# Spreading the loads of x by a plan, and mixing two batches side by side in the first stretch of a fused FFT-mixing and feed-forward kernel

## The chip, the cores and the metric

The kernel runs on one core of one Trainium2 chip. Times are device microseconds (us) of one execution. PE is TensorE (matmul), DVE is VectorE, ACT is ScalarE, POOL is GpSimd, and SP is SyncE, which here only issues DMAs. PE writes its results to buffers in a memory called PSUM; an eviction is the copy out of such a buffer by ACT or DVE. The granted clock is the share of PE's full clock in the trace's clock record; half clock means 0.5.

## The reference, cut to what matters

```python
# x (8, 3008, 256); filt_r, filt_i (1505, 256); w_in (256, 2048); w_out (2048, 256); beta (2048,)
X = np.fft.rfft(x, axis=1)                        # along the 3008 positions
y = np.fft.irfft(X * (filt_r + 1j * filt_i), n=3008, axis=1)
h = y.reshape(24064, 256) @ w_in
g = h * (1 / (1 + np.exp(-beta * h)))             # Swish with a beta per feature
out = g @ w_out                                   # (24064, 256) f32
```

## The kernel before: the parts that the change and the argument touch

The feed-forward part is a loop of 47 blocks of 512 tokens times 16 slices of the hidden width: 752 steps. The mixing (the FFT filter, done as matmuls with tables) of batch b+1 is woven into the steps of the "stretch" in which batch b goes through the feed-forward. Stretch 0 is the first 80 steps. A plan says which step runs which piece.

```python
for s in range(len(steps) + LAG):                 # LAG = 2
    ... two matmuls hps <- y, win_sb (512 columns each); ACT: gT = Silu(hps)
    if s in plan:
        for go in plan[s]: go()                   # pieces of the mixing
    ... four matmuls acc <- gT, wout_sb of step s - LAG; after the last slice DVE copies acc, SP writes out
```

A batch's mixing has four parts, and between them the data goes out to DRAM and comes back in another order:

```python
def s1(b, i, on_act):          # 16 pieces: x times table t1, evicted, written to DRAM scratch d1
    ...
    evac(s["a1"][:, jj : jj + 2, :], ps[:KP], on_act)      # on ACT or on DVE
    if jj + 2 == JG:
        nc.sync.dma_start(s["d1r"][:, g * JG : (g + 1) * JG, :], s["a1"][:])
        if g == J // JG - 1 and b + 1 < B:
            xs[b + 1] = load_x(b + 1)             # 8 DMAs, issued by POOL: the next batch's x
def a2_read(b): ...            # d1 read back as a2, 4 DMAs of 384 KB
def s23(b, i): ...             # 14 pieces, 12 with a product with a2; 4 DVE multiplies; POOL adds p_t + q_t -> v_t;
                               # two pieces later the matmul with v_t, evicted by ACT to z, written to d2
def zz_read(b): ...            # d2 read back as zz, 4 DMAs of 384 KB
def last(b, g, i, on_act): ... # batches 0 and 1: zz times table t4 -> y (s4 and y_read for later batches)
```

The plan of stretch 0 (batch 1 is mixed, batch 2 is begun) and of the later ones:

```python
if w_ == 0:
    place(w_, 0.00, 0.125, u1(b, True), per=2)
    ...
    place(w_, 0.175, 0.175, [lambda b=b: a2_read(b)], per=9)
    place(w_, 0.275, 0.76, u23(b), True)          # True: keep off the borders of blocks
    ...
        place(w_, 0.77, 0.88, u1(b + 1, True), per=2)
    place(w_, 0.80, 0.80, [lambda b=b: zz_read(b)], per=9)
    spread(first_step[1] - 8, first_step[1] - 2, last_units(1, 0))
        at(first_step[1] - 3, lambda b=b: a2_read(b + 1))
else:
    place(w_, 0.03, 0.48, u23(b), True)
    place(w_, 0.525, 0.525, [lambda b=b: zz_read(b)], per=9)
        place(w_, 0.49, 0.63, u1(b + 1))
        ...
```

So x of the next batch is loaded as soon as the last mixing piece `s1` of this batch has been planned. That is just when `d1` is being written and read back, or `d2` is.

## Time and profile before

| | before |
|---|---|
| median of 4 runs | 823.24 us (820.24 to 823.55) |
| span of the profiled execution | 821.0 us |
| PE busy | 782.2 us (95%) |
| one feed-forward step, from the timeline | 0.87 us, times 752 = about 654 us |
| share of PE in the chain that ended last | 80% |

In these traces PE works in order, so a matmul that waits holds up all that follow: four `acc` matmuls stand behind the waiting one at 67.48 us in the timeline below. With PE this busy and its work unchanged, time can only be won where PE stands still or runs at half clock. Idle time of another engine matters only where PE waits for that engine.

The page's 40 slices (each about 20.5 us), kernel before. A digit is the busy share in tenths; PEclk is the granted clock in tenths, and DMA the mean busy share of the 16 DMA engines.

```profile
## 2 busy tenths in 40 slices
PE   7898897999899999999999999999999999999997
...
PEclk9999999999999999999999999999999999999999
DMA  9955239224971349722695128942287033450101
```

The DMA row has a peak in each stretch of about five slices. Between the peaks it falls to 1 to 3.

Who PE waited for, from 39.5 to 800 us, kernel before. Columns: the waiting instruction's tile and line, what released it, total us, times, longest us.

```profile
engine line waited for: us in total, times, longest us
PE ps_2998 L608 <- DMA zz<-d_1773: 3.8, 1, 3.8
PE ps_1159 L551 <- DMA a_1040<-d_805: 2.8, 1, 2.8
PE ps_2098 L551 <- DMA a_2020<-d_1772: 2.4, 1, 2.4
PE ps_1387 L583 <- POOL v_t L573: 2.0, 1, 2.0
PE ps_5539 L608 <- DMA zz<-d_4070: 1.7, 1, 1.7
PE ps_2005 L479 <- DMA zz<-d_806: 1.4, 1, 1.4
```

The three longest waits are for tiles that come back from DRAM: `zz` (line 608) and `a2` (line 551; the profile calls its tiles a_...). The fourth is for POOL's add of `v_t`.

The timeline of PE around the wait at 67.5 us, kernel before. Columns: start, duration (us), engine, line, operation; idle before it and what ended it stand in brackets.

```profile
64.36 0.33 PE L479 MATMUL ps_1153<-t_82,zz 96*128 96x94 bf16 x4
67.48 0.39 PE L551 MATMUL ps_1159<-a_1040,tx 128*128 128x256 bf16 x2 [2.79 <-DMA a_1040<-d_805]
67.71 0.84 PE L782 MATMUL acc<-wout_sb,gT 128*128 128x256 bf16 x4
68.34 1.06 PE L754 MATMUL hps<-y,win_sb 128*128 128x512 bf16 x2
```

After 2.79 us of standing, four `acc` matmuls take 0.84 us and then two `hps` ones 1.06 us. Elsewhere these groups take 0.60 and 0.59. The clock record of the trace says 0.5 for 3.41 us from 67.94 on, and again from 143.03 and from 211.30, at the waits that end at 142.6 and 211.5.

Why the tile is late is in the list of DMA issues, 36 to 72 us, kernel before. Columns: what, queue, count, size of one, us from issue to landing.

```profile
xg<-in_x_dram POOLq DMA_DIRECT2D x4, 320.0 KB, 7.8
...
a_1040<-d_805 SPq DMA_DIRECT2D x1, 384.0 KB, 10.1
```

A read-back of 384 KB takes over 10 us while POOL's load of x runs beside it. The Trainium skill, "DMA: Bandwidth & Descriptors", section "Issuing engines are not separate DMA queues", says that DMAs issued by different engines run on the same 16 DMA engines and interleave. This trace agrees: the two come from different queues (SP and POOL), and the same read for batch 2 takes 3.15 us for its first tile, issued at 139.4, after the last part of x for batch 3 has landed (136.3).

### The profile page before, as it was taken

The page shows a single profiled execution, that of the slowest core. Times are in us where ns is not written, and L with a number is a line of the kernel's source. Part 1 is how long each engine was busy: PE and PEld are TensorE (multiplying, and loading weights), DVE is VectorE, ACT ScalarE, POOL GpSimd, SP SyncE. Part 2 cuts the span into 40 slices and gives each one's busy share as a digit, 9 for nine tenths or more (in the row PEclk, how much of TensorE's full clock was granted, in tenths as well). Part 3 has the DMA queues.
Part 4 walks back from the last instruction along what each step waited for, and adds up shares of the span by engine and source line. Part 5 has one row for each costly group of instructions (what it writes and reads, how often), then busy time and mean ns, then how long its engine had stood idle before and what let it go on. Part 6 is the DMA issues. An engine that isn't in the chain of part 4 may idle for free.

```text
span 821.0 us, 14878 instructions
## 1 busy us (share of the span) xinstructions
PE 782.2 (95%) x5718; PEld 544.9 (66%) x5806; DVE 461.5 (56%) x702; ACT 600.0 (73%) x915; POOL 169.4 (21%) x195
## 2 busy tenths in 40 slices
PE   7898897999899999999999999999999999999997
PEld 4765665766467666777567766676666766666664
DVE  7845962796527966188553877458772792510101
ACT  6786786787477875778667886678767788677775
POOL 8471321232002320034100332013200231000000
PEclk9999999999999999999999999999999999999999
DMA  9955239224971349722695128942287033450101
GB/s 195 232 151 139 64 97 269 81 84 85 271 202 34 102 86 286 183 72 65 148 304 129 46 65 207 279 95 65 74 250 201 26 105 101 130 127 26 52 26 52
DMA packets 125224, 106.94 MB, mean 130 GB/s; under 512 B 41297, under 2 KB 111202, under 8 KB 125154
## 3 DMA queue, kind: packets, MB, share of 16 engines
q1 hardware_dynamic: 120066, 91.05, 37.9%
q0 software_dynamic: 5088, 14.95, 10.2%
q8 instruction: 45, 0.74, 0.4%
q14 instruction: 25, 0.20, 0.1%
HBM read 54.01 MB, written 56.10 MB: 134 GB/s over the span
## 4 chain that ended last, share of the span: by engine, by line
PE 80%; DMA 7%; DVE 6%; issue 2%; POOL 2%; ACT 2%; SPq 0%; DVEq 0%; POOLq 0%; ACTq 0%
PE acc L782 37%; PE hps L754 33%; DVE p_t L564 2%; DVE ost L794 1%; DMA d_1772<-a_1894 1%; DMA a_1040<-d_805 1%; POOL v_t L573 1%; DMA d_5338<-a_5341 1%; DVE q_t L572 1%; DMA d_4069<-a_4072 1%; DMA d_6604<-a_6607 1%; DMA zz<-d_1773 1%; DVE q_t L570 0%; PE psz L399 0%; DMA d_805<-a_942 0%
## 5 line engine op out<-in xcount | busy, mean ns | idle before, releaser
L763 ACT ACTIVATE gT<-hps,beta_sb 128x512 bf16<-128x512 f32 x752 | 516.7, 687 | 198.5 <-PE hps L754 176.1
L782 PE MATMUL acc<-wout_sb,gT 128*128 128x256 bf16 x3008 | 455.1, 273 | 3.2
L754 PE MATMUL hps<-y,win_sb 128*128 128x512 bf16 (+7 forms) x1641 | 431.5, 352 | 0.3 <-DVE y L98 0.2
L782 PEld LDWEIGHTS <-gT 128*128 128x128 bf16 x3008 | 291.8, 98 | 153.9 <-issue 2.8
L573 POOL TENSOR_TENSOR v_t<-p_t,q_t 128x512 bf16<-128x512 f32 x84 | 106.6, 1269 | 411.1 <-DVE q_t L572 383.0
L754 PEld LDWEIGHTS <-win_sb 128*128 128x128 bf16 x1728 | 165.6, 98 | 25.5 <-issue 1.1
L794 DVE COPY ost<-acc 128x512 f32<-128x512 f32 x94 | 60.4, 684 | 211.5 <-PE acc L782 211.5
L108 POOL DMA_DIRECT2D xg<-in_x_dram x32 | 17.9, 561 | 90.6 <-PE ps_3010 L525 8.8
L551 PEld LDWEIGHTS <-tx 128*128 128x128 bf16 x168 | 15.9, 98 | 19.7 <-DMA a_1040<-d_805 2.9
L608 PEld LDWEIGHTS <-t_82 96*96 96x96 bf16 x96 | 11.9, 124 | 20.0 <-DMA zz<-d_1773 4.2
L583 PEld LDWEIGHTS <-t_84 128*128 128x128 bf16 x168 | 15.7, 98 | 12.4 <-issue 5.7
L525 PEld LDWEIGHTS <-t_81 94*96 94x96 bf16 x112 | 13.9, 124 | 12.8 <-issue 0.7
L109 POOL DMA_DIRECT2D xg<-in_x_dram x32 | 16.5, 517 | 3.5 <-DMA win_sb<-in_moe_w_in_dram 3.5
L135 POOL TENSOR_SCALAR wout_sb<-ws,rbeta_sb 128x256 bf16<-128x256 f32 x16 | 14.5, 926 | 5.6 <-DMA ws<-in_moe_w_out_dram 5.6
L479 PEld LDWEIGHTS <-zz 96*128 96x128 bf16 x128 | 8.7, 100 | 10.0 <-issue 2.4
L173 PE MATMUL pw<-wz 128*128 128x512 bf16 x27 | 9.9, 490 | 1.2 <-DVE n_p_i L159 1.2
L94 ACT ACTIVATE z_t<-psz 128x512 bf16<-128x512 f32 x11 | 6.3, 601 | 2.2 <-PE psz L399 2.2
L94 ACT ACTIVATE a_t<-psa 128x384 bf16<-128x384 f32 x12 | 4.9, 475 | 3.7 <-PE psa L267 3.7
L399 PEld LDWEIGHTS <-pb_t 128*128 128x128 bf16 x96 | 5.9, 98 | 1.4 <-DVE pb_t L373 0.8
L399 PE MATMUL psz<-t_84,pb_t 128*128 128x128 bf16 x48 | 6.2, 219 | 0.6 <-DVE pb_t L373 0.6
L399 PE MATMUL psz<-t3q,pb_t 128*128 128x128 bf16 x48 | 6.2, 219 | 0.3 <-ACT t_84 L94 0.3
L457 PEld LDWEIGHTS <-z_t 128*96 128x96 bf16 x64 | 4.4, 123 | 2.6 <-ACT z_t L94 1.0
(1106 smaller groups left out, 704.8 us busy)
## 6 DMA issues: line engine op xcount, KB each, us to landing
out_dram<-ost SPq DMA_DIRECT2D x36, 512.0 KB, 3.2
xg<-in_x_dram POOLq DMA_DIRECT2D x32, 320.0 KB, 7.4
dy<-yo SPq DMA_DIRECT2D x24, 384.0 KB, 5.4
ws<-in_moe_w_out_dram SPq DMA_DIRECT2D x4, 512.0 KB, 11.7
out_dram<-ost SPq DMA_DIRECT2D x5, 384.0 KB, 2.8
xg<-in_x_dram POOLq DMA_DIRECT2D x32, 56.0 KB, 7.3
f_sb<-in_filt_i_dram POOLq DMA_DIRECT2D x8, 192.0 KB, 6.4
f_sb<-in_filt_r_dram SPq DMA_DIRECT2D x8, 192.0 KB, 9.8
```

Of the source, the lines that this page charges most:

```text
L108: nc.gpsimd.dma_start(t[:80], xv[:80, js, :])
L109: nc.gpsimd.dma_start(t[80:NP], xv[80:NP, js, :])
L135: nc.gpsimd.tensor_scalar_mul(wout_sb[:, f0 + i, :], ws[:, i, :], rbeta_sb[:, f0 + i : f0 + i + 1])
L399: nc.tensor.matmul(ps[:, dc, 4 * e : 4 * e + 4, :].rearrange("p a j -> p (a j)"), lhsT=pq[i, half][:, 2 * h + e, dc * P : (dc + 1) * P], r ...
L551: nc.tensor.matmul(ps[:, e, :], lhsT=tx[:, k0 + e, 1:3, :].rearrange("p c k -> p (c k)"), rhs=s["a2"][g][:, kk + e, :], start=True, stop=True,
L564: nc.vector.tensor_tensor(p_t[c * M : (c + 1) * M], x_c, f_sb[M:P, k0 : k0 + 2, :], ALU.mult)
L573: nc.gpsimd.tensor_tensor(v_t[:], p_t[:], q_t[:], ALU.add)
L583: nc.tensor.matmul(ps[:, e, :], lhsT=t3[:, k0 + e, :, :].rearrange("p c k -> p (c k)"), rhs=v_t[:, e, :], start=True, stop=True,)
L754: nc.tensor.matmul(hps[:, pos - t0 : pos - t0 + ln], lhsT=win_sb[:, dc, fb * P : (fb + 1) * P], rhs=ys[b][:, dc, n0 : n0 + ln], start=(dc ...
L763: nc.scalar.activation(gT[:, :tn], hps[:, :tn], ACT.Silu, scale=beta_sb[:, fb : fb + 1])
L782: nc.tensor.matmul(acc[tb // 2][:, tb % 2, :], lhsT=gT[:, tb * P : (tb + 1) * P], rhs=wout_sb[:, fb, :], start=(fb == 0 and tb % 2 == 0), ...
L794: nc.vector.tensor_copy(ost[:, 2 * h : 2 * h + n, :], acc[h][:, :n, :])
```

## The change: its intent, and the diff

The intent has three parts:

- The loads of x leave the place where mixing data makes its way through DRAM, and go where the DMA engines are little used.
- In stretch 0, batch 2's first mixing runs side by side with batch 1's products instead of after them. All its evictions then go to ACT.
- In the set-up, the read-outs of the tables move from ACT to DVE and one cast to POOL ("read-outs reassigned").

The diff, cut to its core:

```diff
-    def load_x(b):
+    def load_x(b, groups=range(J // JG)):
...
+    id_f = setup.tile([NFB, NFB], F32, name="id_f", tag="id_f")
+    gp.tensor_copy(id_f[:], ident[:NFB, :NFB])          # was on ACT, later
...
-                i < 4 or i % 2 == 1,                     # evictions of a_t on ACT
+                i < 4 or i == 6,
...
-    for i in range(2):
+    for i in range(4):
         s1_t(i)
...
-    nc.scalar.activation(beta_sb[:], bps[:], ACT.Copy)
+    nc.vector.tensor_copy(beta_sb[:], bps[:])
-    nc.scalar.activation(t4[:, :NP], tp[:], ACT.Copy)
+    nc.vector.tensor_copy(t4[:, :NP], tp[:])             # and its scaling, likewise
...
-            if g == J // JG - 1 and b + 1 < B:
-                xs[b + 1] = load_x(b + 1)
...
+    def x_units(b): ...                                  # four pieces, each loads a quarter of x[b]
...
-            spread(18, 26, turn_units(2) + last_units(0, 2))
-            place(w_, 0.275, 0.76, u23(b), True)
-            spread(42, 58, turn_units(3) + last_units(0, 3))
+            spread(20, 30, turn_units(2) + last_units(0, 2))
+            place(w_, 0.225, 0.775, u23(b), True)
+            spread(42, 60, turn_units(3) + last_units(0, 3))
             if b + 1 < B:
-                place(w_, 0.77, 0.88, u1(b + 1, True), per=2)
-            place(w_, 0.80, 0.80, [lambda b=b: zz_read(b)], per=9)
-            spread(first_step[1] - 8, first_step[1] - 2, last_units(1, 0))
-            if b + 1 < B:
-                at(first_step[1] - 3, lambda b=b: a2_read(b + 1))
+                spread(15, 24, x_units(b + 1))
+                place(w_, 0.35, 0.82, u1(b + 1, True, 1))   # 1: every piece's eviction on ACT
+                at(70, lambda b=b: a2_read(b + 1))
+            at(66, lambda b=b: zz_read(b))
+            spread(first_step[1] - 6, first_step[1] - 2, last_units(1, 0))
         else:
...
+            if b + 1 < B:
+                place(w_, 0.07, 0.4, x_units(b + 1))
```

More of the change, by code (lines that the diff above doesn't have):

```diff
@@ L98, in evac @@
             nc.vector.tensor_scalar_mul(dst, src, scale)
-    def load_x(b):
+    def load_x(b, groups=range(J // JG)):
         xg = []
         xv = x[b].rearrange("(p j) d -> p j d", j=J)
-        for g in range(J // JG):
+        for g in groups:
             t = xpool.tile([NP, JG, D], BF16, name="xg", tag="xg")
@@ L277, in s1_t @@
                 ps[:, dc, :, :KP].rearrange("p j k -> p k j"),
-                i < 4 or i % 2 == 1,
+                i < 4 or i == 6,
             )
         warm(2, pw[:])
-    for i in range(2):
+    for i in range(4):
         s1_t(i)
     bps = spsum.tile([P, NFB], F32, name="bps", tag="s")
-    id_f = setup.tile([NFB, NFB], F32, name="id_f", tag="id_f")
-    nc.scalar.activation(id_f[:], ident[:NFB, :NFB], ACT.Copy)
     nc.tensor.transpose(bps[:], bt[:], id_f[:])
-    nc.scalar.activation(beta_sb[:], bps[:], ACT.Copy)
+    nc.vector.tensor_copy(beta_sb[:], bps[:])
     tiny = setup.tile([P, NFB], F32, name="tiny", tag="tiny")
@@ L292 @@
     nc.tensor.transpose(tp[:], t1[:], ident[:NP, :NP])
-    nc.scalar.activation(t4[:, :NP], tp[:], ACT.Copy)
-    nc.scalar.activation(t4[0:4], t4[0:4], ACT.Copy, scale=0.5)
-    for i in range(2, 4):
-        s1_t(i)
+    nc.vector.tensor_copy(t4[:, :NP], tp[:])
+    nc.vector.tensor_scalar_mul(t4[0:4], t4[0:4], 0.5)
     nc.scalar.activation(tx[:, :, 1, :], u[:], ACT.Sin, scale=TWO_PI)
@@ L653, in place, with x_units, unit, go @@
         return last_at
-    def u1(b, act=False):
+    def x_units(b):
+        def unit(g):
+            def go():
+                xs[b] = xs.get(b, []) + load_x(b, (g,))
+            return go
+        return [unit(g) for g in range(J // JG)]
+    def u1(b, act=False, every=2):
         def unit(i):
@@ L659, in go @@
                     start(b)
-                s1(b, i, act and i % 2 == 1)
+                s1(b, i, act and i % every == every - 1)
             return go
@@ L691 @@
             spread(4, 12, turn_units(1) + last_units(0, 1))
-            place(w_, 0.175, 0.175, [lambda b=b: a2_read(b)], per=9)
-            spread(18, 26, turn_units(2) + last_units(0, 2))
-            place(w_, 0.275, 0.76, u23(b), True)
-            spread(42, 58, turn_units(3) + last_units(0, 3))
+            at(14, lambda b=b: a2_read(b))
+            spread(20, 30, turn_units(2) + last_units(0, 2))
+            place(w_, 0.225, 0.775, u23(b), True)
+            spread(42, 60, turn_units(3) + last_units(0, 3))
             if b + 1 < B:
-                place(w_, 0.77, 0.88, u1(b + 1, True), per=2)
-            place(w_, 0.80, 0.80, [lambda b=b: zz_read(b)], per=9)
-            spread(first_step[1] - 8, first_step[1] - 2, last_units(1, 0))
-            if b + 1 < B:
-                at(first_step[1] - 3, lambda b=b: a2_read(b + 1))
+                spread(15, 24, x_units(b + 1))
[3 more added lines that the diff above has]
+            spread(first_step[1] - 6, first_step[1] - 2, last_units(1, 0))
         else:
```

## The prediction

> **What bounds it now.** The page gives PE 95% busy of 821.0 us; the chain of waits is 80% PE. In the timeline one of 752 feed-forward steps takes 0.87 us, 652 in all. PE runs in order, so what can be won is where it stands. Start-to-start times of PE's matmuls less their column time sum to about 67 us, 12.8 of it before 40 us. The large ones wait for DMA: 2.8 us at 67.5 (first a2 tile of batch 1), 0.8 and 1.4 at 129 and 134 (zz of batch 1), 2.4 at 142.6 (a2 of batch 2), 3.8 at 211.5, then 0.9, 1.7, 0.8 at 311, 409, 507 (zz of batches 2 to 5). After 67, 142 and 211 the granted clock is 0.5 for 3.4 us, which costs about 1.7 us each. The Trainium skill, "TensorE: Matmul & The Clock Gate", Part 1, says that an idle window of some 3.4 us halves the clock; the trace agrees in length, though 2.4 us of idle sufficed. One wait is for POOL: 2.0 us at 86.
>
> **Why.** Each time the load of the next x (3 MB, DMA engines full for about 12 us) lies on top of a write-then-read through DRAM: a2's first tile took 10.1 us from issue at 57.3, against 3.15 at 139.4. The late stretch without an x load (600 us) has no zz wait.
>
> **What the change does.** No arithmetic goes; eight evictions of 0.6 us move from DVE to ACT in the first stretch. Steps:
> 1. x loads to 0.07–0.40 of each stretch, where DMA share is 0.2–0.3; in the first, three of four stand behind v_t adds in POOL's order, so one can meet the a2 read. Gain: zz waits at 211 (3.8, plus 1.7 of clock) and 311–507 (3.4): with drag 9.5 us. An x issue (1.07 us) fits POOL's gap of 1.56 us between v_t adds.
> 2. First a2: products start at step 18 instead of 22, so a tile at about 60 us leaves a wait near 1 us at full clock: gain 4.
> 3. Batch 2's first mixing ends at step 65, a2 is read at 70, not 77: the wait at 142 and its clock go, 4.2.
> 4. zz of batch 1: no x traffic, but its last producer moves from step 60 to 66, the reader from 72 to 74; about 2 us of wait remain: gain 0.5.
> 5. Three consecutive product steps become two: the wait at 86 shrinks, gain 1.5; but three PSUM buffers now serve products, batch 2's mixing and read-outs together, and DVE holds one for 2.8 us: cost 1.5.
> 6. Set-up: PE's waits at 9.2 and 13.4 go; the last a_t eviction ends near 14.2, not 15.6, but the second filter group lands only at 22.0: gain 1.
>
> Sum about 19 us: 804 us, range 797 to 811. Faster by over 2% (806.8) 0.72; within 2% 0.27; slower 0.01.
>
> **What would show it.** No zz wait over 1 us after stretch one; DMA share near 0.4–0.5 early in later stretches; at most one half-clock stretch between 40 and 800 us; first a2 landing 3 to 4 us after issue; first feed-forward matmul near 38.4 us, not 39.4; first-stretch waits for PSUM buffers or v_t under 3 us in total.
>
> **What would make it wrong.** The a2 wait at step 18 passing 2.4 us and halving the clock again; zz of batch 1 standing over 2 us; PSUM sharing stalling PE at each product; ACT (some 90% booked while both batches mix) delaying Silu; x loads colliding with v_t on POOL.

## The result, and the profile after

The changed kernel ran in 808.83 us (median of 4; 807.65 to 810.24) against 823.24. The ratio is 0.9834, with a 95% interval of 0.9806 to 0.9862. Ratios are the mean time of one kernel's runs over that of the other's of the same rounds, so they are not quite the ratio of the quoted medians. The gain is 14.4 us of medians.

The slices, kernel after:

```profile
## 2 busy tenths in 40 slices
PE   7899998999999999999999999999999999999997
...
PEclk9999998999999999999999999999999999999999
DMA  8956337434854467544783447725495124440101
```

DMA peaks are lower and the valleys fuller, as intended. Here are the quiet parts of the third stretch in the windows view, before (239 to 271 us) and after (228 to 261 us). The last three figures of each row are granted clock, DMA share and GB/s.

```profile
core 0: us, PE busy (x) PEld busy (x) DVE busy (x) ACT busy (x) POOL busy (x), PEclk, DMA share, GB/s
239.00:271.00 32.00, 31.41 (x254) 23.49 (x255) 19.01 (x28) 25.23 (x38) 6.34 (x5) 1.00 0.29 82
```

```profile
228.00:261.00 33.00, 32.57 (x264) 24.09 (x262) 19.47 (x29) 26.17 (x40) 8.61 (x10) 1.00 0.47 108
```

The DMA share rises from 0.29 to 0.47 there. The waits of PE, 39.5 to 800 us, kernel after:

```profile
engine line waited for: us in total, times, longest us
PE ps L477 <- DMA zz<-d: 3.9, 2, 3.0
PE ps L579 <- POOL v_t L569: 2.7, 6, 0.5
PE ps L547 <- DMA a<-d: 1.5, 1, 1.5
PE ps L523 <- ACT z L94: 1.3, 2, 0.9
```

No wait is for `zz` of batches 2 to 5 any more (line 604 in this kernel; line 608 before). The first `a2` wait has gone from 2.8 to 1.5 us. One wait has grown: `zz` of batch 1, at line 477 (line 479 before), from 2.2 us (1.4 and 0.8) to 3.9. In the timeline of PE, kernel after, it looks like this:

```profile
124.11 0.59 PE L761 MATMUL hps<-y,win_sb 128*128 128x512 bf16 x2
127.72 0.34 PE L477 MATMUL ps<-t,zz 96*128 96x94 bf16 x2 [3.01 <-DMA zz<-d]
128.97 0.34 PE L477 MATMUL ps<-t,zz 96*128 96x94 bf16 x2 [0.91 <-DMA zz<-d]
129.10 1.06 PE L789 MATMUL acc<-wout_sb,gT 128*128 128x256 bf16 x4
129.96 1.06 PE L761 MATMUL hps<-y,win_sb 128*128 128x512 bf16 x2
```

PE stands for 3.01 and 0.91 us, and then runs at half clock (1.06 us for a group that takes 0.60). This time the record says 0.5 for 6.83 us, two periods instead of one.

The list of DMA issues, 36 to 72 us, kernel after:

```profile
a<-d SPq DMA_DIRECT2D x4, 384.0 KB, 4.9
...
xg<-in_x_dram POOLq DMA_DIRECT2D x3, 320.0 KB, 4.9
```

The four reads of `a2` now take 4.9 us in the median instead of about 10. The first landed at 60.95, 3.43 us after its issue.

To see where the time came from, I compared the start of the first `acc` matmul of the same step in both timelines:

| at step | before, us | after, us | gained so far | what lies between |
|---|---|---|---|---|
| 0 | 41.95 | 41.50 | 0.46 | set-up |
| 70 | 129.18 | 122.81 | 6.37 | first a2 wait, v_t wait, one zz wait of the kernel before |
| 76 | 136.46 | 135.74 | 0.72 | zz of batch 1: the changed kernel stands and runs cold |
| 84 | 148.56 | 143.67 | 4.89 | a2 of batch 2 |
| 136 | 204.29 | 199.31 | 4.97 | |
| 141 | 215.69 | 205.19 | 10.50 | zz of batch 2 |
| 240 | 316.79 | 305.15 | 11.64 | zz of batch 3 |
| 336 | 415.31 | 401.76 | 13.55 | zz of batch 4 |
| 432 | 512.96 | 498.39 | 14.57 | zz of batch 5 |
| end | 815.57 | 801.04 | 14.52 | |

### The profile page after: what moved, and what is told of

Same layout as the page of the kernel before. It is cut to its first block, busy times and chain, and to the rows that moved or that the text cites. A ratio compares the mean times of both kernels' runs of the same rounds, so it can differ in the third digit from the quotient of the medians.

```text
span 806.5 us, 14967 instructions
## 1 busy us (share of the span) xinstructions
PE 783.2 (97%) x5806; PEld 543.9 (67%) x5806; DVE 457.1 (57%) x699; ACT 602.9 (75%) x917; POOL 169.4 (21%) x196
## 4 chain that ended last, share of the span: by engine, by line
PE 86%; DVE 6%; DMA 3%; POOL 2%; issue 2%; ACT 1%; DVEq 0%; POOLq 0%; SPq 0%; ACTq 0%
PE acc L789 38%; PE hps L761 37%; PE ps L523 3%; PE ps L604 2%; PE ps L579 2%; DVE p_t L560 2%; PE ps L547 2%; DVE ost L801 1%; DMA xg<-in_x_dram 1%; DVE q_t L568 1%; POOL v_t L569 1%; DMA zz<-d 1%; PE ps L477 1%; DMA d<-a 1%; DVE q_t L566 0%
## 5 line engine op out<-in xcount | busy, mean ns | idle before, releaser
L560 DVE TENSOR_TENSOR p_t<-ps,f_sb 64x512 f32<-64x512 f32 x168 | 115.6, 688 | 12.1 <-PE ps L547 8.7
L96 DVE CAST a<-ps 96x512 bf16<-96x512 f32 x88 | 60.0, 686 | 49.5 <-PE ps L523 49.4
L98 DVE TENSOR_SCALAR yo<-ps 96x512 bf16<-96x512 f32 x96 | 65.3, 685 | 36.9 <-PE ps L604 36.8
L568 DVE TENSOR_TENSOR q_t<-ps,f_sb 64x512 f32<-64x512 f32 x84 | 58.2, 693 | 1.1
L566 DVE SCALAR_TENSOR_TENSOR q_t<-ps,f_sb 64x512 f32<-64x512 f32 x84 | 57.4, 683 | 1.2
L94 ACT ACTIVATE z<-ps 128x512 bf16<-128x512 f32 x84 | 49.6, 591 | 1.8 <-PE ps L579 1.8
L523 PE MATMUL ps<-xg,t 94*96 94x512 bf16 x112 | 41.9, 381 | 2.0 <-ACT z L94 1.3
L604 PE MATMUL ps<-zz,t 96*96 96x512 bf16 x96 | 36.6, 381 | 0.0
L579 PE MATMUL ps<-v_t,t 128*128 128x256 bf16 x168 | 32.1, 273 | 3.0 <-POOL v_t L569 2.7
L547 PE MATMUL ps<-a,tx 128*128 128x256 bf16 x168 | 32.1, 273 | 1.5 <-DMA a<-d 1.5
```

The source lines that it names most:

```text
L98: nc.vector.tensor_scalar_mul(dst, src, scale)
L523: nc.tensor.matmul(ps[:KP], lhsT=t1[:], rhs=s["x"][g][:, jj : jj + 2, :], start=True, stop=True)
L547: nc.tensor.matmul(ps[:, e, :], lhsT=tx[:, k0 + e, 1:3, :].rearrange("p c k -> p (c k)"), rhs=s["a2"][g][:, kk + e, :], start=True, stop=True,
L560: nc.vector.tensor_tensor(p_t[c * M : (c + 1) * M], x_c, f_sb[M:P, k0 : k0 + 2, :], ALU.mult)
L568: nc.vector.tensor_tensor(to, x_c, f_i, ALU.mult)
L579: nc.tensor.matmul(ps[:, e, :], lhsT=t3[:, k0 + e, :, :].rearrange("p c k -> p (c k)"), rhs=v_t[:, e, :], start=True, stop=True,)
```

## The experiments

My theory, called X below, was that the whole gain is x traffic leaving the write-then-reads, and that mixing side by side earns nothing. Its rival, M, follows the intent of the change: the gain up to step 84 needs the two batches side by side. A second pair of theories was about the grown `zz` wait: distance between its producer and its reader (D), or contention with other DMA traffic (C). All results were correct.

The runs were made in three sets of rounds, each beside the kernel before: e1 to e4 (its median there was 823.05 us), e5 to e8 (824.24), e9 and after_again (822.34). Only the last set holds the changed kernel too, so other comparisons with it are across rounds.

### Parts of the change alone

**e1_xplan_only**: the kernel before with an x plan alone. In stretch 0 its loads stand at steps 22 to 36; the change has them at 15 to 24, which e8 below tries.

```diff
-            if g == J // JG - 1 and b + 1 < B:
-                xs[b + 1] = load_x(b + 1)
+            spread(22, 36, x_units(b + 1))          # stretch 0
+                place(w_, 0.07, 0.4, x_units(b + 1)) # later stretches
```

> The kernel before with the planned x loads alone, in every stretch (in the first at steps 22 to 36, each behind a v_t add); mixing and set-up as before. Theory X (the gain is x traffic leaving the write-then-reads; mixing side by side earns nothing): waits at 67, 129, 134, 142 and the later zz waits all go, with three half-clock stretches; the wait for v_t near 86 (2.0 us) stays; 802 to 804 us, faster than the whole change. Theory M (mixing the two batches side by side is what earns the 5 us that the change has gained by step 84): only the later zz waits go, about 9.6 us; 812 to 814 us.

Measured: 802.51 us (802.19 to 802.96), ratio 0.9741 (0.9702 to 0.9779). This is theory X's number, and 6.3 us under the median of the whole change. The longest waits of PE from 39.5 to 800 us:

```profile
PE ps L581 <- POOL v_t L571: 4.7, 7, 2.0
PE ps L479 <- ACT z L94: 0.9, 1, 0.9
```

No wait for DMA is left; the first `a2` tile took 3.5 us. The half-clock periods at 67, 142 and 211 are gone, and a new one follows the wait for `v_t` at 80.9 (see below).

**e2_xplan_late_only**: as e1, but x of batch 2 loaded where the kernel before loads it.

```diff
-            if g == J // JG - 1 and b + 1 < B:
-                xs[b + 1] = load_x(b + 1)
+            if g == J // JG - 1 and b == 1:
+                xs[2] = load_x(2)
```

> As the run before it, but the load for batch 2 stays where the kernel before has it, at the end of batch 1's first mixing; planned loads only from the second stretch on. Theory X: the a2 wait at 67 and its half clock stay (about 4.6 us), the waits at 129 to 142 go because the load for batch 3 no longer lies there, later zz waits go; 806 to 808 us. Theory M: 812 to 814 us.

Measured: 804.39 us (803.41 to 806.29), ratio 0.9759 (0.9713 to 0.9805). This is 1.6 us better than the range I gave X, and far from M. The profiled execution, at 806.29 the slowest of the four, has the `a2` wait at 67 with its half clock, and none at 129 to 142 or later. So the load for batch 3, which fell at 118 to 136 us, had made the waits at the end of stretch 0.

**e3_mixing_only**: the changed kernel with x loaded as before (the two added plan lines out, the two removed lines back).

```diff
+            if g == J // JG - 1 and b + 1 < B:
+                xs[b + 1] = load_x(b + 1)
-                spread(15, 24, x_units(b + 1))
-                place(w_, 0.07, 0.4, x_units(b + 1))
```

> The changed kernel with the x loads back where the kernel before has them, at the end of each batch's first mixing; side-by-side mixing and set-up stay. Theory X: the first a2 tile again lands near 66 to 67 us while products now start at step 18, so that wait grows to 6 us or more with half clock; zz of batch 1 waits 4 us or more; later zz waits return; 823 to 830 us. Theory M: about 5 us are kept, 817 to 819 us.

Measured: 829.2 us (825.13 to 831.94), ratio 1.006 (1.0007 to 1.0113): slower than the kernel before, as X had it. Waits of PE, 39.5 to 140 us:

```profile
PE ps L549 <- DMA a<-d: 7.4, 1, 7.4
PE ps L477 <- DMA zz<-d: 7.1, 1, 7.1
```

The two parts add up, within the noise. An x plan alone gives -20.5 us on the medians of these rounds (802.51 against 823.05) and the rest alone +6.2; the sum, -14.4, is what the whole change gives. That the figures meet so closely is partly chance: the four executions of this run spread over 6.8 us, and the x plan of e1 is not quite the change's own.

**e4_setup_only**: the kernel before with the set-up part alone.

```diff
+    id_f = ...; gp.tensor_copy(id_f[:], ident[:NFB, :NFB])   # and ACT's cast out
-                i < 4 or i % 2 == 1,
+                i < 4 or i == 6,
-    for i in range(2): s1_t(i)       # and 2, 3 after the read-outs
+    for i in range(4): s1_t(i)
-    nc.scalar.activation(...)        # beta_sb, t4, t4's scaling
+    nc.vector....
```

> The kernel before with the set-up changes alone (identity cast on POOL, beta and table read-outs on DVE, order of the first mixing, one a_t eviction more on DVE). The changed kernel reached its first output matmul 0.46 us earlier than the kernel before; if the set-up is its own cause this one does too, 41.5 against 41.95 us, and the time is 823 us, the same. If it had fed the later stalls (a2 earlier or later against x traffic), over 1 us.

Measured: 824.87 us (822.94 to 830.92), ratio 1.0024 (0.9969 to 1.0079): the same. The first `acc` matmul came at 41.54 us. That alone would look like the 0.4 us expected. But four kernels with the old set-up (e1, e2, e7, e8) reached it at 41.39, 41.60, 41.34 and 41.33, and those with the new one at 41.44 to 42.06. The kernel before's 41.95 looks like a late execution. The set-up part earns nothing that these traces can show.

### The zz wait of batch 1 in the changed kernel

In the changed kernel batch 1's last product piece runs at step 66 and its reader at step 74, 8 steps apart. In the kernel before they were at 60 and 72. The last `z` write was issued at 118.84 us, just after an output write of 512 KB (118.25) and a mixing write (117.75). It landed at 123.57, and the first `zz` tile only at 127.68, the second at 128.93.

**e5_output_later**: that output write issued three steps later.

```diff
+                if i == 3:
+                    at(s + 3, send)      # send: the loop of output DMAs of this block
+                else:
+                    send()
```

> The changed kernel, with the output write of the fourth block issued three steps later, so that batch 1's last z write and the zz reads no longer share the DMA engines with it. Theory D (the zz wait at 127 in the changed kernel comes from distance: its last producer at step 66, its reader at 74): z write lands about 1 us sooner after its issue (3.5 instead of 4.7), a wait of 2.5 us or more stays; 806 to 809 us. Theory C (contention with the output write makes it): z write lands within 3 us, the wait falls under 2 us with full clock; 802 to 804 us.

Measured: 805.60 us (804.85 to 807.15), ratio 0.9771 (0.9732 to 0.9811). The z write landed 3.2 us after its issue. The wait fell to

```profile
PE ps L477 <- DMA zz<-d: 2.2, 2, 1.1
```

with one half-clock period left. That is between the two expectations: both theories missed, and contention is a part of it.

**e6_producer_early**: the last product piece at step 62.

```diff
-            place(w_, 0.225, 0.775, u23(b), True)
+            place(w_, 0.225, 0.7327, u23(b)[:-1], True)
+            at(62, u23(b)[-1])
```

> The changed kernel with one unit moved: batch 1's last product step goes from step 66 to 62 (where its spacing put it before the rule that keeps block borders free pushed it on). Theory D: z lands about 3.5 us sooner, the zz wait of 4.1 us falls under 1 us and the two half-clock windows (6.8 us, worth about 3) go: 801 to 803 us, level with planned loads alone. Theory C: the output write still lies there, a wait of 2 us or more stays; 805 us or more.

Measured: 806.69 us (804.17 to 807.72), ratio 0.9777 (0.9728 to 0.9826). My expectation for D failed; C's figure held. z landed at 118.49, 5 us sooner than in the changed kernel. But its reads stood in SP's order behind the mixing write (118.79) and the output write (119.29), were issued at 119.85, and the first took 6.1 us beside those two. PE still stood:

```profile
PE ps L477 <- DMA zz<-d: 3.5, 3, 1.9
```

The clock stayed full this time: the wait came in three pieces (0.4, 1.3 and 1.9 us), and none of the clock's periods (see "When a wait costs clock as well") was idle for more than 0.36 of itself.

**e9_zz_clear**: both remedies, and the `zz` reads issued at step 64, ahead of the last mixing write. **after_again**: the changed kernel in the same rounds.

```diff
-            at(66, lambda b=b: zz_read(b))
+            at(64, lambda b=b: zz_read(b))      # plus the edits of the two experiments before
```

> The changed kernel with both remedies for the zz wait of batch 1: its last product at step 62, the zz reads issued ahead of the last mixing write of batch 2 (step 64), and the fourth block's output write three steps later. The two halves alone left 2.5 us and 4.0 us of wait. If distance and other traffic together make the wait, z lands near 118.5 us, the first zz tile within 3.5 us of its issue, PE does not stand at step 74 and no half clock follows: 800.5 to 803 us, 6 to 8 us under the changed kernel run beside it, level with planned loads alone (802.5). If something else holds zz back, 804 us or more.

> The changed kernel as it is, beside the run before it: 808 to 810 us, with the zz waits near 127 and one or two half-clock windows after them.

Measured: 803.22 us (802.18 to 804.03) against 809.81 (808.90 to 811.88) for the changed kernel in the same rounds: 6.6 us less, as expected, though 0.2 us above the range I gave the time. z landed at 118.24, and the first zz tile 4.0 us after its issue (3.5 expected). The two longest waits of PE up to 140 us are now

```profile
PE ps L547 <- DMA a<-d: 2.0, 1, 2.0
PE ps L523 <- ACT z L94: 1.3, 2, 0.9
```

with no wait for zz and no half clock between 40 and 798 us. So the grown wait was made by distance and traffic together: each remedy alone left a part of it. What the earlier issue of the reads does by itself was not run. The 6.6 us are about all that separates the changed kernel from the x plan alone (803.2 against 802.5, in different rounds).

This does not show that mixing side by side costs nothing. e9 still pays for an `a2` wait of 2.0 us, and e1 for a `v_t` wait of 2.0 us and its half clock, which a better spacing takes away (e7, below). From the first `acc` matmul of step 84 to the last one of all, the changed kernel, e1, e7 and e9 each take 657.4 us, so they differ only before it. e7 reaches step 84 at 134.05 us, e9 at 137.27, e1 at 137.69 and the changed kernel at 143.67. No run joined side-by-side mixing with such a spacing and with no wait for `a2`, so what it is worth by itself stays open; in these runs it earned nothing.

### Two questions about the x plan

**e8_xplan_ungated**: e1 with the load of batch 2's x at steps 15 to 24 instead of 22 to 36, so that three of its four parts stand ahead of the first `v_t` add in POOL's order.

```diff
-            spread(22, 36, x_units(b + 1))
+            spread(15, 24, x_units(b + 1))
```

> The kernel with planned x loads alone, but the load for batch 2 at steps 15 to 24, so that three of its four parts stand before the first v_t add in POOL's order and start at once. If it matters that v_t adds hold x loads back, the first a2 tile lands near 65 us instead of 59.8 and the products at step 22 wait 1 to 2 us, without or with half clock: 803 to 806 us. If not, 802.5 us with no wait for a2.

Measured: 802.78 us (801.53 to 805.80), ratio 0.9740 (0.9697 to 0.9783): no cost that shows, the second of the two cases. The three loads were issued at 51.8 to 54.5 and landed by 62.7. The read of `a2` was issued 3.3 us later than in e1, its first tile landed at 63.78, and the products at step 22 came just then. Whether holding x back behind `v_t` matters with the products at step 18, where the changed kernel has them, was not tried.

**e7_xplan_even**: e1 with batch 1's product pieces at least two steps apart.

```diff
-            place(w_, 0.275, 0.76, u23(b), True)
+            for s_, go in zip((22, 25, 28, 31, 34, 37, 40, 43, 45, 50, 52, 55, 58, 61), u23(b)):
+                at(s_, go)
```

> The kernel with planned x loads alone, its batch 1 product steps set at least two steps apart (22, 25, 28, 31, 34, 37, 40, 43, 45, 50, 52, 55, 58, 61) in place of three in a row at 34 to 36. If the 2.1 us wait for v_t at 80.9 and its half-clock window come from three products in a row, both go: 798.5 to 800 us. If POOL or DVE is short over the whole stretch, the waits move elsewhere and the time stays at 802.5.

Measured: 798.95 us (798.91 to 800.09), ratio 0.9692 (0.9654 to 0.9729). As expected, the 2.0 us wait and its half clock go:

```profile
PE ps L581 <- POOL v_t L571: 2.7, 6, 0.5
PE pz L457 <- DVE q_t L570: 0.9, 1, 0.9
```

This is the fastest version: 25 us under the kernel before in the same rounds (median 824.24), and about 10 under the changed one in other rounds. Like e1 it keeps the old order of the two batches and the old set-up. So a plan for x and an even spacing did more than the whole change, without side-by-side mixing.

## Why the prediction was right or wrong, point by point

The time (808.8) lies in the range (797 to 811), but it is 4.8 us above the centre, and "faster by over 2%", to which the prediction gave 0.72, did not come true. There is luck in how well the range held: step 5 below came out about 2 us better than predicted, and without that the time would have been near the range's upper end (an estimate: 808.8 + 2). By term:

| step of the prediction | predicted gain | measured |
|---|---|---|
| 1, later zz waits | 9.5 | 9.6 (5.53 + 1.14 + 1.91 + 1.02 from the table of steps) |
| 2, first a2 | 4 | about 3: 2.8 us of wait and about 1.7 of clock became 1.5 us at full clock |
| 3, a2 of batch 2 | 4.2 | about 4.1: the 2.4 us wait and its half clock are gone |
| 4, zz of batch 1 | 0.5 | about -4.6: see below |
| 5, v_t and PSUM sharing | 0 | about 2: the v_t wait of 2.0 us at 86 is gone, and what came in its place about balances other small waits that left |
| 6, set-up | 1 | 0.46 in this pair of traces, nothing across all traces |

**The main reading was right.** e1 shows that the x loads lying on the write-then-reads made the waits: moving them alone gains 20.5 us, more than the whole change. Step 1 was right to 0.1 us, and the control inside the trace (no zz wait near 600 us, where no x is loaded) had told it.

**Step 4 failed in its size, and in its sign.** It said "about 2 us of wait remain: gain 0.5". From the starts of PE's matmuls, less the column time of the one before, the two zz waits cost 0.9 and 1.5 us in the kernel before, and 3.2 and 1.2 us in the changed one. There the slice from 120 to 140 us has 2.8 us more of excess, which is the half clock. So the term went from 2.5 to 7.1 us. I had counted the z write and the reads at their durations without company (2.8 and 3.15 us in the kernel before; the prediction does not print this sum). The output write and batch 2's last mixing write share those microseconds, and stand ahead in SP's order. The z write took 4.7 us and the first read 4.0, instead of 2.8 and 3.15. And a wait of 4 us pays for the clock as well. The prediction named this as a way to be wrong ("zz of batch 1 standing over 2 us") but gave it too little weight. e9 shows its worth directly: 6.6 us.

**Step 6 failed.** PE's waits at 9.2 and 13.4 did go. Others took their place (0.8 us at 10.7, for the cast that moved to POOL), and the gain at the first `acc` lies within the scatter of executions. "First feed-forward matmul near 38.4" was 38.9.

**Signs that held:** no zz wait after stretch one; DMA share 0.47 early in the third stretch; first a2 landing 3.43 us after its issue; one half-clock stretch between 40 and 800 us, of double length; first-stretch waits for evictions or v_t of about 2 us in total.

**A figure of the prediction that was too large:** the "67 us" by which PE stands. The group lines of the whole run show why, kernel before:

```profile
L782 PE MATMUL acc<-wout_sb,gT 128*128 128x256 bf16 x3008 | 455.1, 273 | 3.2
L754 PE MATMUL hps<-y,win_sb 128*128 128x512 bf16 (+7 forms) x1641 | 431.5, 352 | 0.3 <-DVE y L98 0.2
```

and kernel after:

```profile
L761 PE MATMUL hps<-y,win_sb 128*128 128x512 bf16 (+7 forms) x1728 | 449.2, 352 | 0.2 <-DMA xg<-in_x_dram 0.2
```

The trace of the kernel before lacks 87 of its 1728 `hps` records (it has 5806 weight loads, as the other has, but 88 matmuls fewer than weight loads), and each gap of a missing matmul counted as standing: 87 times 0.217 us is 19 us. The true sum was about 48 us, by this estimate. The terms of the prediction came from single waits, so the error went no further.

### When a wait costs clock as well

e1 and e8 happen to hold a close pair. PE's timeline around the wait for `v_t`, e1:

```profile
80.89 0.54 PE L581 MATMUL ps<-v_t,t 128*128 128x256 bf16 x2 [1.98 <-POOL v_t L571]
81.22 1.06 PE L792 MATMUL acc<-wout_sb,gT 128*128 128x256 bf16 x4
82.07 1.06 PE L764 MATMUL hps<-y,win_sb 128*128 128x512 bf16 x2
```

and e8:

```profile
80.83 0.38 PE L581 MATMUL ps<-v_t,t 128*128 128x256 bf16 x2 [1.98 <-POOL v_t L571]
81.04 0.60 PE L792 MATMUL acc<-wout_sb,gT 128*128 128x256 bf16 x4
81.48 0.59 PE L764 MATMUL hps<-y,win_sb 128*128 128x512 bf16 x2
```

The wait is 1.98 us in both. In e1 the next groups take 1.06 us, in e8 they take 0.60. The clock records suggest why. In all twelve traces (those of the kernels before and after, and of the ten runs) the changes of clock fall on a grid of 3.41 us, whose phase differs from run to run. In e1 the whole wait lies in one cell of the grid (77.6 to 81.0, PE idle for 0.58 of it). In e8 a border at 80.4 cuts it, and no cell is idle for more than 0.46. I worked out the idle share of each cell in all twelve traces. At full clock, all 15 cells that were idle for 0.58 or more were followed by half clock, and none that was idle for 0.51 or less was (some 70 cells between 0.23 and 0.51, about 40 of them after the set-up). That is an observation, and no run was made to test it as a rule.

## What to carry to other kernels

When data goes out to DRAM and straight back, look at what else is on the DMA engines in those microseconds. Here a bulk load without urgency, placed on top, tripled a 3 us read, and moving the load alone gained 2.6%. A change of several parts should be run part by part: here one part earned more than the whole, and the rest took some of it back, mostly through a wait that it had made longer itself. And a write-then-read should be costed with the traffic that is planned beside it and ahead of it in its queue, not with the durations it has alone.

## What the Trainium skill lacked or had wrong

- "TensorE: Matmul & The Clock Gate", Part 1 ("after ≥1 idle window (~3.4µs)") and "Why this matters for your kernels" (no idle gaps over about 3 us): here 1.98 us of standing was enough in e1, where it fell inside one cell of the 3.41 us grid (0.58 of it idle), and was free in e8, where a border cut it. That the window is free-running and 3413 ns long, as the page says, these traces confirm: half-clock stretches end on that grid and last one to three cells (3.41 to 10.24 us).
- The same page, on the way back to full clock: half clock lasted one cell where the cell after the drop was idle for 0.09 of itself or less (8 drops), and two or three where it was idle for 0.17 or more (7 drops; 0.27 in the kernel after). A wait that runs over the border costs more clock: about 2.8 us in the kernel after, not 1.7.
- No page that I looked at says that matmul records can be missing: 1641 of 1728 in the kernel before's trace, 1728 of 1728 in the changed kernel's; the traces of e5 to e8 lack 87 too. A sum of gaps over such a trace is too large (here by about 19 of 67 us).
